# A new order of transposes and VectorE work in the first projection of a fused attention and MLP block, with its backward pass

## The chip, the cores and the metric

The kernel runs on one NeuronCore of a Trainium2 chip. The metric is device time in microseconds (us) of one launch. Engines are named as in the profile: PE is TensorE's matmul and PEld its weight load, DVE is VectorE, ACT is ScalarE, POOL is GpSimd, and SP is SyncE, which here only issues transfers (DMAs).

## The reference

The reference computes a transformer block's output and, from `grad_out`, its gradients (seven outputs in all, bfloat16):

```
h   = x + A(layernorm(x))                 # linear attention, 32 heads of 20
h2  = h + B(layernorm(h))                 # SwiGLU MLP
A:  q, k, v = split(x @ wqkv);  phi(t) = where(t > 0, t + 1, exp(t)) + 1e-6
    o = phi(q) (phi(k)^T v) / (phi(q) sum_s phi(k));  A = o @ wo
B:  (silu(x @ w1) * (x @ w3)) @ w2
```

x is 2048 x 640, wqkv 640 x 1920, wo 640 x 640, w1 and w3 640 x 1728, w2 1728 x 640.

## The kernel before

The 2048 rows are 16 tiles of 128 rows (128 partitions). The 640 columns are 5 blocks of 128 (`DT`), or two halves of 320 (`HD`), since a PSUM bank holds 512 float32. All instructions are written out by hand in each engine's order; an engine takes its own list in order and waits on semaphores. So the order in which lines are called is the order on each engine, and an instruction that waits holds up all that stands behind it on its engine. SP's transfers are also one list in order.

**Stage 1 (0 to 55 us)**, around which the change lies, goes over tiles t = 0 to 15:

- layer norm statistics on DVE (`Stats.part`: two BatchNorm statistics, L147, an aggregate, L150, an addition of epsilon, L153), then 1/sigma on POOL (L154);
- normalization in place: on DVE (L160), or for tiles 10, 12 and 14 on ACT (`norm_act`, L165), which needs a bias that POOL makes (L169, L170);
- the transposed rows `pqT`: for tiles 0 to 7 by five PE transposes into PSUM (L254) and an ACT copy (L256), for tiles 8 to 15 by a transposing DMA on SP (L247);
- the key product, 2 x 5 matmuls of 320 columns into a two-bank PSUM tile "big" (L260), of which there are two buffers;
- phi: Exp (L277) and Relu (L278) on ACT from PSUM, and two DVE operations (L281, L282), put off in the list `held` (the "rest").

Between the tiles stand four query products (`q_tile`, after the tiles in `QT`), four chunks of the MLP's backward product (`ghh_chunk`, 5 matmuls of 512 columns, L371, with an ACT copy, L391), and the accumulation of phi(k)^T x (`m_part`, L402). Before the first rows arrive, PE runs 44 matmuls on ones (L441). Loads are issued in the order of the lines 114, 187 to 193 and 429 to 435: x tiles 0 and 1, two weight blocks, x tiles 2, 3, 4 to 7, then `w2T`, `g2T`, `w2T`, x tiles 8 to 11, the query weights, x tiles 12 to 15. During the loop, stores of keys and normalized rows (`outs`) and MLP weights (`trickle`) go into SP's list too.

**Stage 2 (to about 88 us)** ends the sums, transposes the matrix M by DMA (L414), finishes queries and makes the combined matrix Wp. **Stage 3 (88 to 100 us)** computes the attention output of the tiles 0 to 3 (and 4) in halves: `f2_half(t, j)` is 5 matmuls (L586), for the second half one more with x (L584), an addition on DVE (L591) or a copy on ACT (L589), and the second layer norm's statistics; `f2_hn(t)` normalizes on DVE, `f2_ht(t)` transposes on PE (L677) and copies on ACT. Their order is the list in `run(...)`, lines 801 to 809. After that come the MLP, the backward pass and the weight gradients, up to 825 us, which the change leaves alone.

Of the kernel before, what the change touches and what calls it, by code (L numbers as in the profile page):

```python
# [9 lines left out]
P = 128  # L10
BF16 = mybir.dt.bfloat16
F32 = mybir.dt.float32
ALU = mybir.AluOpType
AF = mybir.ActivationFunctionType
# [4 lines left out]
S, D, H, F = 2048, 640, 32, 1728  # L19
DH = D // H  # L20
ST, DT = S // P, D // P
# [3 lines left out]
HD = D // 2  # L25
# [30 lines left out]
def kernel(  # L56
# [51 lines left out]
    cp = pool("cp")  # L108
# [4 lines left out]
    x_sb = x_ext[:, :, 0:D]  # L113
# [16 lines left out]
    class Stats:  # L130
# [25 lines left out]
        def center(self, out, src, t):  # L156
            V.tensor_scalar(out=out, in0=src, scalar1=self.mv[:, t, 0:1], scalar2=None, op0=ALU.subtract)
# [4 lines left out]

        def norm_act(self, out, src, t):

            A.activation(out=out, in_=src, func=AF.Identity, bias=self.nb[t][:, 1:2], scale=self.rs[:, t:t + 1])  # L165

        def bias(self, t):
            nb = self.nb[t] = cp.tile([P, 2], F32, name="nb", bufs=4)
            G.tensor_tensor(out=nb[:, 0:1], in0=self.mv[:, t, 0:1], in1=self.rs[:, t:t + 1], op=ALU.mult)  # L169
            G.tensor_tensor(out=nb[:, 1:2], in0=zero[:], in1=nb[:, 0:1], op=ALU.subtract)  # L170

    ln1, ln2 = Stats("ln1"), Stats("ln2")

# [7 lines left out]
    def load_wq(a, b):  # L181
        dma(out=wqkv[:, :, a * HD:b * HD], in_=wq_v[:, :, a * HD:b * HD])

    def load_x(a, b):
        dma(out=x_sb[:, a:b, :], in_=xS[:, a:b, :])

    load_x(1, 2)
    A.activation(sg[:], zero[:], AF.Exp)
    load_wq(2, 3)
    load_wq(3, 4)  # L190
    load_x(2, 3)
    load_x(3, 4)
    load_x(4, 8)

# [26 lines left out]
    def load_g2T(c):  # L221
        g2T[c] = U2.tile([P, DT, W], BF16, name="g2T", tag="g2T", bufs=2)
        dmaT(out=g2T[c][:], in_=goD[c * W:(c + 1) * W, :])

    def load_w13(c0, c1):
        def go1():
            dma(out=w1[:, c0:c1, 0:F], in_=rows(B_w1)[:, c0:c1, :])

        def go3():
            dma(out=w3[:, c0:c1, :], in_=rows(B_w3)[:, c0:c1, 0:F - FL])  # L230
        return [go1, go3]
# [3 lines left out]
    Z = cp.tile([P, DT], F32, name="Z")  # L235

    XT_DMA = 8
    WARM = 44

    def on_act(t):  # L240
        return t > XT_DMA and t % 2 == 0

    def p1_norm(t):
        xn = x_sb[:, t, :]
        (ln1.norm_act if on_act(t) else ln1.norm)(xn, xn, t)
        if t >= XT_DMA:
            dmaT(out=pqT[:, :, t * P:(t + 1) * P], in_=xn)  # L247

    def p1_tr(t, parts=((0, DT),)):
        xn = x_sb[:, t, :]  # L250
        for a, b in parts:
            tr = ps.tile([P, DT, P], BF16, name="tr", bufs=2)
            for c in range(a, b):
                T.transpose(tr[:, c, :], xn[:, c * P:(c + 1) * P], ident[:])  # L254

            A.copy(out=pqT[:, a:b, t * P:(t + 1) * P], in_=tr[:, a:b, :])  # L256

    def p1_half(acc, t, n0):
        for c in range(DT):
            T.matmul(acc, lhsT=pqT[:, c, t * P:(t + 1) * P], rhs=wqkv[:, c, n0:n0 + HD], start=(c == 0),  # L260
                     stop=(c == DT - 1))

    def p1_mm(t, n0):
        acc = ps.tile([P, 2, 512], F32, name="big", bufs=2)
        for j in range(2):
            p1_half(acc[:, j, 0:HD], t, n0 + j * HD)
        return acc

    def two(ap):
        return ap.rearrange("p (j n) -> p j n", j=2)  # L270

    held = []

    def phi(acc, dst, then=None):

        mq, rq = (p1.tile([P, D], BF16, name=n, bufs=b) for n, b in (("mq", 3), ("rq", 3)))
        A.activation(two(mq[:]), acc[:, :, 0:HD], AF.Exp)  # L277
        A.activation(two(rq[:]), acc[:, :, 0:HD], AF.Relu)  # L278

        def rest():  # L280
            V.tensor_scalar(out=mq[:], in0=mq[:], scalar1=1.0, scalar2=1e-6, op0=ALU.min, op1=ALU.add)  # L281
            V.tensor_tensor(out=dst, in0=mq[:], in1=rq[:], op=ALU.add)  # L282
            if then is not None:
                then()
        held.append(rest)

    def phi_rest(keep=0):
        while len(held) > keep:
            held.pop(0)()
# [13 lines left out]

    def q_tile(t):
        q_home(t)
        phi(p1_mm(t, 0), pqs[t])

    dz = {}

# [65 lines left out]
    def ghh_chunk(n, acc):  # L375

        c, fc = divmod(n, FT)
        if fc == FT - 1:
            gh, hw = ghh[n // 2], W // 2
            G.memset(gh[FL:, 1, :], 0.0)  # L380
            for d in range(DT):
                for h in range(2):
                    T.matmul(acc[h * FL:(h + 1) * FL, 0:hw], lhsT=w2T[:, d, fc * P:fc * P + FL],
                             rhs=g2T[c][:, d, h * hw:(h + 1) * hw], start=(d == 0), stop=(d == DT - 1))
            for h in range(2):
                A.copy(out=gh[:FL, 1, h * hw:(h + 1) * hw], in_=acc[h * FL:(h + 1) * FL, 0:hw])
            return
        mm5_to(acc, w2T, fc, g2T[c])
        if n % 2 == 0:
            ghh[n // 2] = pf.tile([P, 2, W], BF16, name="ghh", bufs=4)  # L390
        A.copy(out=ghh[n // 2][:, n % 2, :], in_=acc[:])  # L391
# [37 lines left out]
    def load_w2T(a, b):  # L429
        dmaT(out=w2T[:, :, a:b], in_=B_w2[a:b, :])  # L430

    zero_pads()
    load_w2T(0, 2 * P)
    load_g2T(0)
    load_w2T(2 * P, 4 * P)
    load_x(8, 12)
    load_wq(0, 2)
    load_x(12, ST)
    warm = ps.tile([P, 512], F32, name="warm", tag="tr", bufs=2)
    for _ in range(WARM):  # L440
        T.matmul(warm[:, 0:P], lhsT=ones[:], rhs=ones[:], start=True, stop=True, skip_group_check=True)  # L441
    ln1.run(x_sb, 0, 1)
    ln1.part(x_sb, 1, 0)
    for a, b in ((0, 2 * P), (2 * P, D)):
        ln1.norm(x_sb[:, 0, a:b], x_sb[:, 0, a:b], 0)
    p1_tr(0, ((0, 2), (2, DT)))
    for t in (1, 2):
        if t == 1:
            ln1.part(x_sb, t, 1)
            p1_norm(t)  # L450
            ln1.run(x_sb, t + 1, t + 2)
        else:
            ln1.part(x_sb, t + 1, 0)
            p1_norm(t)
    ln1.part(x_sb, 3, 1)
    w13 = [go for c0, c1 in ((0, 2), (2, 4), (4, 5)) for go in load_w13(c0, c1)]
    w13 += [lambda: dma(out=w1[:, :, F:FP], in_=rows(B_w3)[:, :, F - FL:F])]

    def load_wo():
        dma(out=wo[:], in_=A_wo.rearrange("(c p) n -> p c n", p=P))  # L460

    trickle = {3: w13[0], 4: w13[1], 11: lambda: load_wq(4, 6), 12: w13[2], 14: w13[3], 15: load_wo}

    stat_of = {t: (t + 4,) for t in range(7)}
    stat_of.update({7: (11, 12), 8: (13,), 9: (14,), 10: (15,)})
    norm_of = {t: (t + 3,) for t in range(8)}
    norm_of.update({8: (11, 12), 9: (13,), 10: (14,), 11: (15,)})

    def xn_out(g, q):
        sl = slice(g * TPC, (g + 1) * TPC)  # L470
# [3 lines left out]
        sl = slice(g * TPC, (g + 1) * TPC)  # L474
        dma(out=pk_v[:, sl, :], in_=pk_all[:, sl, :])

    outs = {6: ((group_out, 0),), 7: ((xn_out, 0, dma),), 10: ((group_out, 1), (xn_out, 1, dma)), 13: ((group_out, 2),)}

    QT = (5, 7, 9, 11)
    for t in range(ST):  # L480
        k = p1_mm(t, D)
        if t < 3:
            p1_tr(t + 1, ((0, 2), (2, DT)))
        for n in stat_of.get(t, ()):
            ln1.run(x_sb, n, n + 1)
            if on_act(n):
                ln1.bias(n)
        for n in norm_of.get(t, ()):
            if not on_act(n):
                p1_norm(n)  # L490
        phi_rest(t < 4)
        phi(k, pk_all[:, t, :])
        for n in norm_of.get(t, ()):
            if on_act(n):
                p1_norm(n)
        if t in QT:
            q_tile(QT.index(t))
        if 2 <= t < 6:
            ghh_chunk(t - 2, ps.tile([P, 2, 512], F32, name="gp", tag="big", bufs=2)[:, 0])
            p1_tr(t + 2)  # L500
        if t >= 3:
            m_part(0, [t - 3])
        if t >= 11:
            V.memset(bd[:, t - 11, :], 0.0)
            make_mask(t - 11)
        if t >= 9:
            m_part(1, [2 * (t - 9), 2 * (t - 9) + 1])
        for f, *n in outs.get(t, ()):
            f(*n)
        if t in trickle:  # L510
            trickle[t]()
# [285 lines left out]
    def kv3():  # L797
# [4 lines left out]
        (q_late, 12, lambda: (f2_wT(0), f2_wT(1))), (q_late, 13, lambda: (f2_wT(2), f2_wT(3))), (phi_rest,),  # L802
        (q_late, 14, lambda: f2_wT(4)), (load_x, 4, 8), (r_head, 5), (r_prod, 7), (r_store, 5, 6), (f2_m_out,),
        (f2_w_out,), (q_out, 8, 10), (q_out, 10, 14), (load_w2T, 8 * P, 10 * P), (mlp_ghh, 4), (q_late, 15),
        (sig_table,), (f2_half, 0, 0), (f2_half, 1, 0), (f2_half, 0, 1), (f2_half, 1, 1), (f2_hn, 0), (mlp_ghh, 5),
        (f2_half, 2, 0), (f2_hn, 1), (load_w2T, 10 * P, F), (f2_half, 2, 1), (f2_ht, 0), (f2_half, 3, 0), (f2_hn, 2),
        (f2_half, 3, 1), (f2_ht, 1), (mlp_ghh, 6), (f2_hn, 3), (f2_ht, 2), (r_red, 6), (r_inv, 6), (r_scale, 6), (r_T, 6),
        (f2_half, 4, 0), (f2_ht, 3), (mlp_ghh, 7), (f2_half, 4, 1), (r_red, 7), (r_inv, 7), (r_scale, 7), (r_T, 7),
        (r_store, 6, 8))
    p1.release()  # L810
# [623 lines left out]
```

## Time and profile before

| what | value |
|---|---|
| median of 5 runs | 826.6 us (826.46 to 827.25) |
| profiled execution, its own time | 826.57 us |
| its span (first to last instruction) | 824.8 us |
| PE busy | 817.1 us, 99% of the span |
| DVE, ACT, POOL busy | 453.7, 318.9, 134.1 us |
| PE busy in 0:5, 5:10, 10:15, 15:20 us | 3.88, 4.42, 3.70, 5.00 us |
| PE busy in 70:80, 80:90, 90:100 us | 9.77, 9.72, 9.19 us |
| granted PE clock | 0.999 of full speed |

The page's busy times are sums over one profiled execution. The windows give the busy time of each engine in a stretch, counted from the start of the span. A line of the timeline holds the start, the length, the engine, the line of the kernel, the operation, what it writes and reads, how often, and in brackets the idle time of the engine before it with what ended it. A "SPq" line is the issue of a transfer, not the transfer itself; the transfer view gives the time from issue to landing.

### The profile page before, as it was taken

The numbers are of one execution on the slowest core, as the hardware profiler recorded it, in microseconds if no ns is written. First come the engines' busy times: TensorE is split into PE (matmuls) and PEld (weight loads), VectorE is DVE, ScalarE is ACT, GpSimd is POOL, SyncE is SP. The second block draws the span as 40 slices with busy tenths as digits, with TensorE's granted clock in tenths as the row PEclk, the third lists the DMA queues.
The fourth block names the chain that finished last, engine by engine and source line by source line (L and its number), as shares of the span: only waits on it lengthen the run. The fifth ranks groups of instructions, "written<-read, shape, count | busy, mean of one in ns | idle before, by whom it ended". The sixth has DMA issues, their size and how long they took to land.

```text
span 824.8 us, 14217 instructions
## 1 busy us (share of the span) xinstructions
PE 817.1 (99%) x5551; PEld 523.0 (63%) x5551; DVE 453.7 (55%) x960; ACT 318.9 (39%) x609; POOL 134.1 (16%) x196
## 2 busy tenths in 40 slices
PE   8999999999999999999999999999999999999998
PEld 5677644555555555777777777777777777555554
DVE  7859897999898566300057777772681545200000
ACT  5855787655655666011121212222212334211111
POOL 2334343223323212100001111110220000000000
PEclk9999999999999999999999999999999999999999
DMA  9899999696484555999878889258995788985781
GB/s 265 206 319 210 247 243 283 201 237 170 123 223 128 151 190 167 214 248 265 222 166 182 193 214 200 59 111 178 247 235 93 164 189 176 217 201 132 162 173 38
DMA packets 318338, 157.58 MB, mean 191 GB/s; under 512 B 235456, under 2 KB 311456, under 8 KB 318272
## 3 DMA queue, kind: packets, MB, share of 16 engines
q1 hardware_dynamic: 286256, 120.65, 63.5%
q0 software_dynamic: 7376, 24.81, 8.9%
q10 hardware_dynamic: 24640, 11.23, 6.6%
q8 instruction: 43, 0.70, 0.4%
q14 instruction: 23, 0.19, 0.1%
HBM read 48.15 MB, written 51.46 MB: 121 GB/s over the span
## 4 chain that ended last, share of the span: by engine, by line
PE 94%; DMA 2%; DVE 1%; SPq 1%; ACT 1%; POOL 1%; issue 0%; DVEq 0%; ACTq 0%
PE mm L371 20%; PE job L1198 19%; PE ghn L1000 14%; PE gxn L1356 8%; PE o L766 7%; PE gw L955 7%; PE big L260 3%; PE gwo L1085 3%; PE gr L1057 3%; PE dkv L1302 3%; PE macc L402 2%; PE at L586 2%; DMA g2T<-in_grad_out_dram 1%; DMA mT<-mbs 1%; PE dkv L1230 1%; PE gp L371 1%
## 5 line engine op out<-in xcount | busy, mean ns | idle before, releaser
L1198 PE MATMUL job<-gb,hnN 128*128 128x432 bf16 (+2 forms) x656 | 117.0, 342 | 0.0
L1000 PEld LDWEIGHTS <-ggb 128*128 128x128 bf16 x864 | 84.5, 98 | 32.8
L1198 PEld LDWEIGHTS <-hnN 128*128 128x128 bf16 x656 | 63.6, 98 | 53.4
L371 PE MATMUL mm<-pqT,w 128*128 128x512 bf16 x405 | 93.6, 379 | 0.0
L371 PEld LDWEIGHTS <-w 128*128 128x128 bf16 x540 | 52.5, 98 | 62.9 <-issue 0.8
L1202 ACT CAST obs<-job 128x432 bf16<-128x432 f32 (+3 forms) x61 | 29.3, 480 | 123.1 <-PE job L1198 123.1
L766 PE MATMUL o<-w,hhT 128*128 128x320 bf16 x448 | 67.5, 299 | 0.0
L1000 PE MATMUL ghn<-w13a,ggb 128*128 128x320 bf16 x448 | 63.5, 299 | 0.0
L1000 PE MATMUL ghn<-w13b,ggb 128*128 128x320 bf16 x416 | 61.4, 299 | 0.0
L371 PE MATMUL mm<-g2T,w2T 128*128 128x512 bf16 x240 | 59.6, 379 | 0.0
L766 PEld LDWEIGHTS <-hhT 128*128 128x128 bf16 x448 | 43.8, 98 | 23.6
L955 PE MATMUL gw<-g,hb 128*128 128x320 bf16 x416 | 56.8, 299 | 0.0
L1065 POOL TENSOR_TENSOR sz<-Zb,g_h 128x640 f32<-128x640 bf16 x16 | 20.2, 1260 | 199.4 <-DVE g_h L1063 199.4
L955 PEld LDWEIGHTS <-hb 128*128 128x128 bf16 x416 | 40.6, 98 | 16.0 <-issue 0.3
L1356 PE MATMUL gxn<-wqT,gT 128*128 128x320 bf16 x320 | 48.7, 299 | 0.0
L391 ACT CAST ghh<-mm 128x512 bf16<-128x512 f32 x48 | 28.2, 588 | 46.9 <-PE mm L371 41.4
L705 ACT ACTIVATE sig<-mm 128x512 bf16<-128x512 f32 x56 | 33.5, 599 | 27.3 <-PE mm L371 23.9
L1012 ACT ACTIVATE gs<-ghn 128x640 bf16<-128x640 f32 x16 | 11.2, 703 | 79.1 <-PE ghn L1000 79.1
L371 PEld LDWEIGHTS <-w2T 128*128 128x128 bf16 x260 | 25.3, 98 | 24.6 <-issue 1.4
L260 PE MATMUL big<-wqkv,pqT 128*128 128x320 bf16 x260 | 39.5, 299 | 0.9 <-ACT pqT L256 0.6
L260 PEld LDWEIGHTS <-pqT 128*128 128x128 bf16 x320 | 30.4, 98 | 14.1 <-ACT pqT L256 2.1
L1356 PEld LDWEIGHTS <-gT 128*128 128x128 bf16 x320 | 31.3, 98 | 12.2
(201 smaller groups left out, 1283.0 us busy)
## 6 DMA issues: line engine op xcount, KB each, us to landing
hh_d<-hhT SPq DMA_DIRECT2D x24, 256.0 KB, 2.6
gg_d<-gate POOLq DMA_DIRECT2D x24, 256.0 KB, 4.0
gg_d<-ghh POOLq DMA_DIRECT2D x24, 256.0 KB, 3.4
ggb<-gg_d SPq DMA_DIRECT2D x6, 896.0 KB, 5.5
ggb<-gg_d SPq DMA_DIRECT2D x6, 832.0 KB, 7.0
x_sb<-in_A_x_dram SPq DMA_DIRECT2D x7, 640.0 KB, 6.1
out_dram<-obs ACTq DMA_DIRECT2D x39, 108.0 KB, 3.2
ggb<-gg_d SPq DMA_DIRECT2D x2, 1728.0 KB, 13.2
```

The source lines that it names most:

```text
L260: T.matmul(acc, lhsT=pqT[:, c, t * P:(t + 1) * P], rhs=wqkv[:, c, n0:n0 + HD], start=(c == 0), stop=(c == DT - 1))
L371: T.matmul(acc[:], lhsT=w[:, c, fc * P:(fc + 1) * P], rhs=rhs[:, c, :], start=(c == 0), stop=(c == DT - 1))
L391: A.copy(out=ghh[n // 2][:, n % 2, :], in_=acc[:])
L705: A.activation(sig[:, i, :], gp[:], AF.Sigmoid)
L766: T.matmul(o2["ps"][:, 0:HD], lhsT=hhT[c][:, fc, i * P:(i + 1) * P], rhs=w2[:, fc, j * HD:(j + 1) * HD], start=(fc == 0), stop=(fc == FT - 1))
L955: T.matmul(acc[:, j, 0:HD], lhsT=hb[b][:, t, i * P:(i + 1) * P], rhs=g2[:, t, j * HD:(j + 1) * HD], start=(t == 0), stop=(t == ST - 1))
L1000: T.matmul(acc[:, j, 0:HD], lhsT=ggb[t // 2][:, k, lo:lo + P], rhs=rhs[:, j * HD:(j + 1) * HD], start=(k == 0), stop=(k == NG - 1))
L1057: T.matmul(gr[t][:, j, 0:HD], lhsT=ghT[t][:, c, :], rhs=wT2[:, c, j * HD:(j + 1) * HD], start=(c == 0), stop=(c == DT - 1))
L1085: T.matmul(acc[m][:, j, 0:n], lhsT=r_sb[:, t, m * P:(m + 1) * P], rhs=g_hx[:, t, j * HD:j * HD + n], start=(t == 0), stop=(t == ST - 1))
L1198: T.matmul(acc[:, 0:n], lhsT=lhs[:, t, m * P:(m + 1) * P], rhs=rhs(t), start=(t == 0), stop=(t == ST - 1))
L1202: A.copy(out=ob, in_=acc[:, 0:n])
L1356: T.matmul(acc[:, j, 0:HD], lhsT=g, rhs=wqT[:, k, j * HD:(j + 1) * HD], start=(k == 0), stop=(k == 14))
```

## The change

It does the following, in the order of the program:

1. x tile 2 is loaded before the second weight block, x tiles 8 to 11 before the second part of `w2T`.
2. 34 instead of 44 matmuls on ones at the start, and 8 more between the transposes and the product of tile 0.
3. Tile 0 is only centered at first (`RAW = 1`), 256 columns on DVE and 384 on ACT; its 1/sigma is applied as the scale of Exp and Relu, and to the rows themselves later (`("C", 0)` at step 3).
4. The transposes of tile t + 1 stand between the two halves of the key product of tile t, and are copied in one piece.
5. DVE's work in the loop follows a written list `v_steps`: S is statistics, N a normalization (A one on ACT), R the oldest put-off rest of phi, C the scaling of tile 0.
6. The chunks of the MLP's backward product move from the steps 2 to 5 to the steps 3 to 6, and into the PSUM banks of tag "m"; `m_part(0, ...)` starts at step 7 with tiles 0 to 2.
7. The second stores of keys and of rows go out at step 12 instead of 10, behind the last transposing DMAs; the first MLP weights one step later; the first query product at step 6.
8. The bias for normalization on ACT is one POOL instruction instead of two.
9. In stage 3, the first halves of the tiles 0 to 2 come first, and all halves of the tiles 0 to 3 before the first transposes.

```diff
-            G.tensor_tensor(out=nb[:, 0:1], in0=self.mv[:, t, 0:1], in1=self.rs[:, t:t + 1], op=ALU.mult)
-            G.tensor_tensor(out=nb[:, 1:2], in0=zero[:], in1=nb[:, 0:1], op=ALU.subtract)
+            G.tensor_scalar(out=nb[:], in0=self.mv[:, t, 0:1], scalar1=self.rs[:, t:t + 1], scalar2=-1.0, op0=ALU.mult,
+                            op1=ALU.mult)
...
+    load_x(2, 3)
     load_wq(3, 4)
-    load_x(2, 3)
...
-    WARM = 44
+    WARM = 34
+    RAW = 1
...
+    def p1_scale(t):
+        xn = x_sb[:, t, :]
+        V.tensor_scalar(out=xn, in0=xn, scalar1=ln1.rs[:, t:t + 1], scalar2=None, op0=ALU.mult)
...
+    def p1_mm(t, n0, between=None):
+        acc = p1_acc()
         for j in range(2):
             p1_half(acc[:, j, 0:HD], t, n0 + j * HD)
+            if j == 0 and between is not None:
+                between()
...
+        kw = dict(scale=ln1.rs[:, t:t + 1]) if t < RAW else {}
+        A.activation(two(mq[:]), acc[:, :, 0:HD], AF.Exp, **kw)
+        A.activation(two(rq[:]), acc[:, :, 0:HD], AF.Relu, **kw)
...
+    load_x(8, 12)
     load_w2T(2 * P, 4 * P)
-    load_x(8, 12)
...
+    def center_first():
+        V.tensor_scalar(out=nmean[:], in0=ln1.mv[:, 0, 0:1], scalar1=-1.0, scalar2=None, op0=ALU.mult)
+        center(0, 0, 2 * P)
+        A.activation(out=x_sb[:, 0, 2 * P:], in_=x_sb[:, 0, 2 * P:], func=AF.Identity, bias=nmean[:, 0:1])
...
+    ln1.part(x_sb, 0, 0)
+    ln1.part(x_sb, 0, 1, center_first)
     p1_tr(0, ((0, 2), (2, DT)))
+    warm_up(8, p1_acc()[:, 0])
+    stat(1)
+    ln1.part(x_sb, 2, 0)
+    p1_norm(1)
+    ln1.part(x_sb, 2, 1)
+    ln1.part(x_sb, 3, 0)
+    p1_norm(2)
+    ln1.part(x_sb, 3, 1)
+    ln1.part(x_sb, 4, 0)
+    p1_norm(3)
+    ln1.part(x_sb, 4, 1)
...
-    trickle = {3: w13[0], 4: w13[1], 11: lambda: load_wq(4, 6), 12: w13[2], 14: w13[3], 15: load_wo}
+    trickle = {4: w13[0], 5: w13[1], 11: lambda: load_wq(4, 6), 12: w13[2], 14: w13[3], 15: load_wo}
+    R = None
+    v_steps = {1: (R, ("N", 4)), 2: (("S", 5), R, ("N", 5)), 3: (("S", 6), R, ("N", 6), ("C", 0)),
+               4: (("S", 7), R, ("N", 7), ("S", 8)), 5: (R, ("N", 8), ("S", 9)), 6: (R, ("N", 9), ("S", 10)),
+               7: (("S", 11), R, R, ("A", 10), ("N", 11)), 8: (("S", 12), R, R, ("S", 13), ("A", 12)),
+               9: (("N", 13), R, ("S", 14)), 10: (R, R, ("S", 15), ("A", 14)), 11: (("N", 15), R)}
...
-    outs = {6: ((group_out, 0),), 7: ((xn_out, 0, dma),), 10: ((group_out, 1), (xn_out, 1, dma)), 13: ((group_out, 2),)}
-    QT = (5, 7, 9, 11)
+    outs = {6: ((group_out, 0),), 7: ((xn_out, 0, dma),), 12: ((group_out, 1), (xn_out, 1, dma)), 13: ((group_out, 2),)}
+    QT = (6, 7, 9, 11)
+    M0 = {7: (0, 1, 2), 8: (3, 4, 5)}
+    M0.update({t: (t - 3,) for t in range(9, ST)})
     for t in range(ST):
-        k = p1_mm(t, D)
-        if t < 3:
-            p1_tr(t + 1, ((0, 2), (2, DT)))
+        k = p1_mm(t, D, (lambda: p1_tr(t + 1)) if t + 1 < XT_DMA else None)
...
-        if 2 <= t < 6:
-            ghh_chunk(t - 2, ps.tile([P, 2, 512], F32, name="gp", tag="big", bufs=2)[:, 0])
-            p1_tr(t + 2)
-        if t >= 3:
-            m_part(0, [t - 3])
+        if 3 <= t < 7:
+            ghh_chunk(t - 3, ps.tile([P, 512], F32, name="gp", tag="m", bufs=2))
+        m_part(0, M0.get(t, ()))
...
-        (sig_table,), (f2_half, 0, 0), (f2_half, 1, 0), (f2_half, 0, 1), (f2_half, 1, 1), (f2_hn, 0), (mlp_ghh, 5),
-        (f2_half, 2, 0), (f2_hn, 1), (load_w2T, 10 * P, F), (f2_half, 2, 1), (f2_ht, 0), (f2_half, 3, 0), (f2_hn, 2),
-        (f2_half, 3, 1), (f2_ht, 1), (mlp_ghh, 6), (f2_hn, 3), (f2_ht, 2), (r_red, 6), (r_inv, 6), (r_scale, 6), (r_T, 6),
+        (sig_table,), (f2_half, 0, 0), (f2_half, 1, 0), (f2_half, 2, 0), (f2_half, 0, 1), (f2_half, 1, 1), (f2_hn, 0),
+        (f2_half, 2, 1), (f2_half, 3, 0), (f2_half, 3, 1), (f2_ht, 0), (f2_hn, 1), (mlp_ghh, 5), (load_w2T, 10 * P, F),
+        (f2_hn, 2), (f2_ht, 1), (mlp_ghh, 6), (f2_hn, 3), (f2_ht, 2), (r_red, 6), (r_inv, 6), (r_scale, 6), (r_T, 6),
```

## The prediction

> **What bounds the kernel now.** I read the page's busy times first, then TensorE's waits over the whole run, then the windows in which the change acts.
>
> ```profile
> PE 817.1 (99%) x5551; PEld 523.0 (63%) x5551; DVE 453.7 (55%) x960; ACT 318.9 (39%) x609; POOL 134.1 (16%) x196
> ...
> PE   8999999999999999999999999999999999999998
> ```
>
> TensorE (PE) is busy 817.1 of 824.8 us. So only its 7.7 us of idle time, and work taken from it, can be won. About 1.1 us lie before its first matmul and 3.3 us behind its last, and the change touches neither. The rest, about 3.3 us, lies in two places, which the windows show (the column behind the length is PE's busy time):
>
> ```profile
> 5.00:10.00 5.00, 4.42 (x37) 2.47 (x35) 3.70 (x12) 2.42 (x6) 1.21 (x3) 1.00 1.15 310
> 10.00:15.00 5.00, 3.70 (x28) 1.89 (x27) 4.79 (x16) 4.28 (x9) 1.91 (x3) 1.00 1.13 237
> 15.00:20.00 5.00, 5.00 (x40) 3.40 (x39) 4.61 (x16) 3.55 (x6) 1.36 (x2) 1.00 0.99 344
> ...
> 90.00:100.00 10.00, 9.19 (x72) 5.87 (x72) 8.22 (x25) 5.55 (x12) 4.78 (x8) 1.00 0.98 294
> ```
>
> From 100 to 800 us PE has no idle at all: what is won before 100 us reaches the end. The timeline of PE names the stalls:
>
> ```profile
> 6.30 1.96 PE L260 MATMUL big<-wqkv,pqT 128*128 128x320 bf16 x10
> 8.09 0.44 PE L254 MATMUL tr<-ident,x_sb 128*128 128x128 bf16 x5
> 8.83 1.64 PE L260 MATMUL big<-wqkv,pqT 128*128 128x320 bf16 x10 [0.30 <-ACT pqT L256]
> 10.31 0.45 PE L254 MATMUL tr<-ident,x_sb 128*128 128x128 bf16 x5
> 11.05 1.64 PE L260 MATMUL big<-wqkv,pqT 128*128 128x320 bf16 x10 [0.30 <-ACT pqT L256]
> ...
> 14.15 1.24 PE L371 MATMUL gp<-g2T,w2T 128*128 128x512 bf16 x5 [0.98 <-DMA g2T<-in_grad_out_dram]
> ```
>
> The reader sees a key product (10 matmuls) start every 2.22 us, because each waits for ScalarE (ACT) to copy its transposed rows, and then a wait for g2T. A matmul's modelled record outlives its issue, so I count by starts: 0.136 us a 320-column matmul, 0.056 a transpose, 0.215 a 512-column one, which are the steps between starts here.
>
> **Part 1: the first tile.** Before, VectorE (DVE) waits for GpSimd's 1/sigma (0.57 us) and normalizes at 5.14. Now it only subtracts the mean, at about 4.4 behind the aggregate (4.06 + 0.21), 0.31 us for 256 columns as in L160's half: 4.7. The 34 remaining warm-ups end at 1.12 + 34 x 0.107 = 4.75. The other 384 columns go to ACT, an operation without a row: between 0.42 (128x320 cast) and 0.92 us (L165, 128x640); I take 0.64. Copies of the transposes end near 6.1 (6.4 at the upper end). Nothing is won: the first weights were issued at 1.73 and land 4.5 us later, at 6.24, and the product began at 6.30 for that reason. It begins at 6.30 again; the 8 new fillers lie in that wait, cost 0.
>
> The spacing of the 44 warm-ups in the trace is 0.107 us for 34 steps and 0.056 after 4.8 us. The Trainium skill, "TensorE: Matmul & The Clock Gate", Part 1, says that the gate opens after about 3.4 us of activity in a free-running window, give or take 0.5 us, and not after a count; that speaks against a fixed 34. By it, a gate open 0.5 us late would slow two transposes and the fillers, all still before 6.30: the sum stays.
>
> **Part 2: tiles 1 to 3.** The load of x tile 2 moves ahead of the second weight block. It landed at 7.80 (issue 2.76 + 5.0); the step from a tile's landing to the next is 0.44, so I put it at 6.24 + 0.43 = 6.67 and the weights at 7.80 (before 7.38). This matters, since in DVE's order half of tile 2's statistics now stand ahead of tile 1's normalization: statistics 6.73, norm 7.13 to 7.57, transposes of tile 1 at 7.62 (inside product 0), second half 7.90 to 8.58, ACT's 640-column copy (0.70) to 8.82, product 1 at 8.88 (before 8.83). From there a tile costs one loop: half a product 0.68, transposes 0.28, their drain 0.17, copy 0.70, two handovers of 0.05: 1.93 against 2.22. Products 2 and 3 start at 10.82 and 12.76; product 3 with its transposes ends at 14.40. The chunk that waited for g2T (it lands at 14.02) is now behind product 3 and waits no more: it ends at 15.48. Before, the same work (products 0 to 3, transposes 1 to 4, one chunk) was issued by 15.51 + 1.36 = 16.87. **Won: 1.39 us.**
>
> **Part 3: tiles 4 to 15.** PE's work is the same, only ordered anew. Two waits of before, 0.23 at 24.4 and 0.32 at 32.56 us (weight loads held by the PSUM buffer that ACT still read), lie in this stretch. New is this: ACT's normalization of tiles 10, 12 and 14 stands right behind the Exp and Relu of keys 7, 8 and 10, and its statistics come only one step earlier in DVE's list. For tile 12: its statistics started at 29.57 and now stand behind two more finishing pairs (0.32 + 0.49 each) and norm 11 (0.36), all 1.39 earlier: 30.2. They take 1.3 with the epsilon, 1/sigma 0.55 to 32.1, bias 0.40 to 32.5, then 0.92 on ACT; Exp and Relu of key 9 (0.60 apart, 0.70 each) end at 34.72. They are queued behind it, and product 10 needs their PSUM buffer: it starts at 34.76, where PE is ready at 34.35. Tile 14 does the same to product 12: 0.27. With 0.08 at query 0, new waits are 0.76 against 0.55. Product 12 starts at about 40.75 against 41.82: **1.07 won so far.**
>
> The bias is now one GpSimd tensor-scalar, which no row shows: 0.19 and 0.40 are the rows of a 128x1 tensor-tensor there, 1.26 that of 128x640. I take 0.40, the nearest under load. At 0.19 all these waits shrink by about 0.2 in sum; at 1.26 they cost some 1.0 more.
>
> The transfers of tiles 8 and 9: before, w1 lands at 14.66 + 11.9 = 26.6 and w3 at 15.88 + 12.8 = 28.7; a transposed row transfer takes about 0.6 behind them. Tile 8's now stands ahead of w3: 27.2 against product 8 at 28.6. Tile 9's stands behind it: 29.9 against 30.8. Both covered, the second by 0.9. The second stores of keys and rows leave the queue at step 10 and come after the four last transposes: nobody reads them before 100 us; but the weights behind them (w1, w3, wo) then start with as much ahead of them as before. The scaling of row tile 0 (0.44 on DVE at step 3) lies under the chunk.
>
> **Part 4: 50 to 88 us** is unchanged work, one stretch of it waiting on a transfer:
>
> ```profile
> 61.37 2.07 SPq L414 DMA_TRANSPOSE mT<-mbs  x1
> 63.55 2.60 SPq L361 DMA_TRANSPOSE pqT<-pq  x1
> 66.20 3.06 SPq L430 DMA_TRANSPOSE w2T<-in_B_w_dram  x1
> 69.36 2.85 SPq L361 DMA_TRANSPOSE pqT<-pq  x2
> 72.31 2.06 SPq L414 DMA_TRANSPOSE mT<-mbs  x1
> ```
>
> SP issues these back to back up to the mT transfer that PE waits for at 78.16 (0.23 us). The first started on data (ACT's copy ended at 61.34), and SP was free at 60.75: it can come 0.62 earlier, not 1.07. So between 0 and 0.45 is given back; I take 0.2.
>
> **Part 5: attention halves.** The order becomes 0a 1a 2a 0b 1b 2b 3a 3b, then the transposes. Third a-half (0.68) covers the wait for Wp (0.28 at 89.89). Worked on the old clock: halves from 87.96, four of 0.68 and four of 0.816: 93.94; transposes of row 0 and a chunk to 95.30. DVE is the slow side: adds at 88.84, 89.77, 90.70 (0.93 each with its statistics), then statistics of 0 and 1, norm 0 at 93.29, statistics of 2, add of 3 at 94.46, statistics to 96.28, and only then norm 1 (0.43), which stood at 94.51 before: 96.63. PE waits 1.38 there, and is at row 3's transposes at 99.00. Before:
>
> ```profile
> 99.05 0.45 PE L677 MATMUL trh<-ident,hn 128*128 128x128 bf16 x5 [0.81 <-DVE hn L160]
> ```
>
> Won: 0.05. The stalls move, their sum hardly changes.
>
> **Sum.** 1.07 - 0.2 + 0.05 = 0.9, taken from the profiled execution's own 826.57 us (span 824.8 and 1.8 around it; the median of the five runs is 826.6, so the two agree): 825.6 us.
>
> **Rivals.** *More is won* (824.6): GpSimd is faster in the waits of part 3 (0.55 and 0.19 us, rows that stand where DVE is not in its fast copies), which removes most of 0.76, and mT moves with PE. *Nothing* (825.6 + 1.1 = 826.7): x tile 2 lands as late as before, 7.80. Then product 1 starts at 10.0, 1.1 later, as DVE's order puts tile 1 behind it. For it: wide weight rows share all DMA engines; against: loads landed in issue order. A bias of 1.26 gives the same (826.6). *Slower* (827.4): the clock. PE is idle 0.3, 0.5 and 0.6 us between 4.75 and 7.62, and the fast warm-ups of before are gone; if the clock fell to half for one stretch as long as the first, 3.6 us, it would lose 1.8. It decides when matmuls between 6.3 and 10 us start 0.27 apart instead of 0.136. Against: before, the clock stayed up through 1.2 us without a matmul start (12.95 to 14.15). *The change does not do what it says*: if tile 1's transposes wait past the second half, the loop stays at 2.22, 0.9 is lost: counted under nothing.
>
> **Chances.** Forecast (825.0 to 826.0) 0.40; more (825.0 and below) 0.36; nothing (826.0 to 827.0) 0.15; slower (827.0 and up) 0.09. The range 824.0 to 827.2 takes in the bounds of the bias, of mT and of the late tile. The line at 0.2% (1.65 us, about what a measurement of this kernel can tell from no change) lies at 824.95 and 828.25: faster is the "more" case, 0.36; slower is most of the last, 0.07; within, 0.57.
>
> **What would show it.** Product 1 near 8.9 and then starts 1.9 apart; no wait for g2T; ACT idle about 1 us ahead of the norms of 12 and 14, and a wait of 0.4 and 0.3 at products 10 and 12; PE's largest wait at the second attention transposes, 1.4. Wrong if product 1 starts after 9.5, if the matmuls before 10 us are half as fast, or if PE waits for pqT transfers or over 0.7 for mT.

## The result, and the profile after

The changed kernel is slower: 827.03 us (median of 44 runs, 825.37 to 838.0) against 826.86 (79 runs, 826.0 to 835.0). The ratio of the mean times, without the slowest run, is 1.0030, 95% interval 1.0017 to 1.0042; the 0.2% that the forecast called measurable lies inside that interval. The median hides the shape: 27 runs lie at 825.4 to 827.9 us with a median of 826.3, 0.6 us under the kernel before, and 17 lie at 831.7 to 838.0, around 834.7. Before, one of the 79 runs was over 830.

The profiled run is one of the lower group: 825.76 us, span 824.0. Its busy time, and the windows that were shown of before (the column behind the length is PE's busy time):

```profile
PE 816.4 (99%) x5549; PEld 523.2 (63%) x5549; DVE 453.5 (55%) x961; ACT 320.6 (39%) x607; POOL 133.5 (16%) x193
```

```profile
5.00:10.00 5.00, 4.05 (x39) 2.83 (x38) 3.89 (x13) 2.55 (x6) 1.54 (x3) 1.00 1.17 299
10.00:15.00 5.00, 4.32 (x37) 2.84 (x35) 4.45 (x16) 4.97 (x8) 1.37 (x3) 1.00 1.06 239
15.00:20.00 5.00, 5.00 (x39) 3.20 (x37) 4.76 (x15) 4.48 (x9) 0.99 (x3) 1.00 1.09 305
...
90.00:100.00 10.00, 8.75 (x68) 5.55 (x67) 9.40 (x28) 5.61 (x11) 4.12 (x7) 1.00 1.02 315
```

From 5 to 20 us PE is busy 0.25 us longer than before, from 90 to 100 us 0.44 shorter. PE's timeline shows the places:

```profile
6.06 0.84 PE L265 MATMUL big<-wqkv,pqT 128*128 128x320 bf16 x5
7.34 0.45 PE L255 MATMUL tr<-ident,x_sb 128*128 128x128 bf16 x5 [0.44 <-DVE x_sb L160]
8.24 1.52 PE L265 MATMUL big<-wqkv,pqT 128*128 128x320 bf16 x10 [0.44 <-DMA wqkv<-in_A_wqkv_dram]
...
11.29 0.85 PE L265 MATMUL big<-wqkv,pqT 128*128 128x320 bf16 x5 [0.58 <-ACT pqT L257]
...
14.86 1.24 PE L380 MATMUL gp<-g2T,w2T 128*128 128x512 bf16 x5
```

```profile
95.95 0.45 PE L701 MATMUL trh<-ident,hn 128*128 128x128 bf16 x5 [1.25 <-DVE hn L160]
...
98.28 0.44 PE L701 MATMUL trh<-ident,hn 128*128 128x128 bf16 x5
```

The chunk of g2T waits no more. In the attention one wait of 1.25 us at the second row's transposes stands in place of the two of before, and the fourth row's transposes start at 98.28 instead of 99.05. So this run shows what was forecast (825.6). Part of that is luck: it is the third fastest of the 44, and its group's median lies 0.6 us under the kernel before, not the 0.9 of the forecast. The result is decided by something that it does not show: the upper group.

### The profile page after: what moved, and what is told of

Same layout as the page of the kernel before. It is cut to its first block, busy times and chain, and to the rows that moved or that the text cites. A ratio compares the mean times of both kernels' runs of the same rounds, so it can differ in the third digit from the quotient of the medians.

```text
span 824.0 us, 14214 instructions
## 1 busy us (share of the span) xinstructions
PE 816.4 (99%) x5549; PEld 523.2 (63%) x5549; DVE 453.5 (55%) x961; ACT 320.6 (39%) x607; POOL 133.5 (16%) x193
## 4 chain that ended last, share of the span: by engine, by line
PE 96%; DVE 2%; ACT 1%; DMA 1%; issue 0%; SPq 0%; POOL 0%; DVEq 0%; ACTq 0%
PE mm L380 20%; PE job L1222 19%; PE ghn L1024 14%; PE gxn L1380 8%; PE o L790 7%; PE gw L979 7%; PE big L265 3%; PE gwo L1109 3%; PE gr L1081 3%; PE dkv L1326 3%; PE macc L411 2%; PE at L610 2%; PE mm L265 1%; DMA wqkv<-in_A_wqkv_dram 1%; DVE st L147 1%; PE dkv L1254 1%
```

## The experiments

Kernels were run beside the kernel before, which stayed at 826.0 to 829.4 in 129 of its 134 runs there; the other five took 830.4 to 836.0, so it knows long runs too, but rarely. Sixteen runs in three theories follow.

**First theory: the clock at the start.** The upper group's mean granted clock is 0.993 to 0.998. PE is idle in places between 4.75 and 8.2 us, so full speed might be granted late. Four runs tell this from the two rivals (the new 1.25 us wait, the order of the loads).

```diff
-    WARM = 34
+    WARM = 44
```

> The changed kernel with 44 instead of 34 matmuls on ones. Of the 44 runs of the changed kernel 27 took 825.4 to 827.9 us and 17 took 831.7 to 838.0 with a mean granted clock of 0.993 to 0.998. Theory (start clock): full speed is granted only after a stretch of dense PE work, and with 34 matmuls on ones the idle places from 4.75 to 8.2 us fall into that stretch in part of the runs. Then ten more fill it to about 5.8 us and no run takes over 830; median 826.3, within 0.4 us of the changed kernel's undisturbed runs, since the first 1.0 us of them lies in the wait for tile 1's rows. Rival A (the new 1.25 us wait of PE at 96 us lets the clock fall): 4 of 10 runs stay at 834 to 835. Rival B (loads in another order, the idle places at 7 and 8 us alone): also 4 of 10 stay.

Measured: 830.64 us (828.2 to 832.8, 9 runs), ratio 1.0043 (1.0029 to 1.0057). The opposite: no run under 828.

```diff
-    WARM = 34
+    WARM = 24
```

> The changed kernel with 24 instead of 34 matmuls on ones. Theory (start clock): PE has idle time from 3.7 us on, so nearly all runs (over 7 in 10) take 832 or more, and the trace shows PE at half speed behind 5 us for a long stretch, some 8 us lost in all. Rival A (wait at 96 us) and rival B (idle places at 7 and 8 us): 4 in 10 as in the changed kernel, median near 826.5 or 834 by luck; by A the half-speed stretch stands behind 95 us, by B between 8 and 20 us.

Measured: 826.8 to 835.2, 7 of 12 over 830. In the profiled run (828.5 us, not one of the seven) full speed begins at 4.3 us and stays.

Old order of the halves, the list of `run(...)` as before:

```diff
-        (sig_table,), (f2_half, 0, 0), (f2_half, 1, 0), (f2_half, 2, 0), (f2_half, 0, 1), (f2_half, 1, 1), (f2_hn, 0),
+        (sig_table,), (f2_half, 0, 0), (f2_half, 1, 0), (f2_half, 0, 1), (f2_half, 1, 1), (f2_hn, 0), (mlp_ghh, 5),
...
```

> The changed kernel with the order of the attention halves of before. Theory (start clock): still about 4 in 10 runs at 832 or more; the others at 826.2 to 826.4, 0.1 us either way of the changed kernel, since the waits there only moved (forecast 0.05 us for the order; the trace shows 1.25 us at row 1 against 0.28 and 0.81 before). Rival A (the new 1.25 us wait at 96 us drops the clock): no run over 830.

Measured: 8 of 12 over 830. The order of the halves is not the cause. The profiled run, 832.6 us, fell into the upper group and ended the theory: full speed from 4.2 us, then a wait of 5.11 us for the normalization of row tile 3 (DVE, L160) at 98 us, and behind it one stretch of half speed, from 103.15 us, 3.41 long.

And the kernel before with fewer matmuls on ones:

```diff
-    WARM = 44
+    WARM = 34
```

> The kernel before with 34 instead of 44 matmuls on ones, nothing else changed. Theory (start clock): its PE is then idle from 4.77 to 5.5 us, so runs at 832 or more appear here too, fewer than in the changed kernel since its first product starts at 6.3 and runs through to 8.1: 1 to 4 in 10; the others at 826.8. Rivals A and B: none, all 826.0 to 828.0 but for 2 in 79.

Measured: 827.2 us, 1 of 12 over 830: as before, within what can be told (ratio 1.0004, 0.9981 to 1.0027).

**Second theory: a late transfer.** `f2_hn(3)` writes its rows into a buffer of tag "pql", the one that query tile 5 (`pql`) left. Its transposing transfer to `pqT` (issued on SP, L370) must have read it first. In the trace of before it landed at 97.48 us and the normalization started at 98.54, so nothing waited. In the run with the old order of the halves it landed at 102.42. The changed kernel again, as it is:

> The changed kernel once more on the chip of the other runs, to see both of its groups beside them: about 6 in 10 runs at 825.4 to 827.9 and 4 in 10 at 832 to 838. If the profiled run falls into the upper group, late transfer theory: tile 3's normalization on VectorE stands still for over 3 us up to a landing of the query transfer behind 100 us, and the half-clock window follows it; start clock theory (already doubtful): half speed before 20 us.

Measured: 8 of 12 over 830 (833.5 us). The profiled run is of the upper group, 835.49 us. Its VectorE and PE timelines, and the tile view of pqT from 86 to 106 us (who waited for it, and the time from issue to landing):

```profile
94.77 0.80 DVE L160 TENSOR_SCALAR hn<-x_sb,ln_mv,ln_rs 128x640 bf16<-128x640 bf16 x2
105.00 0.45 DVE L160 TENSOR_SCALAR hn<-x_sb,ln_mv,ln_rs 128x640 bf16<-128x640 bf16 x1 [9.43 <-DMA pqT<-pql]
```

```profile
96.92 0.84 PE L610 MATMUL at<-Wp,pqT 128*128 128x320 bf16 x5
105.51 0.72 PE L701 MATMUL trh<-ident,hn 128*128 128x128 bf16 x5 [7.75 <-DVE hn L160]
106.02 2.34 PE L380 MATMUL mm<-g2T,w2T 128*128 128x512 bf16 x5
```

```profile
  DVE hn L160: 9.4, 1
...
DMA to landing us min/median/max: 16.7/16.7/16.7
```

The transfer takes 16.7 us instead of 7.2 (lower group) and 8.1 (before). The windows of PE behind it (busy, then granted clock, DMA share, GB/s):

```profile
100.00:103.00 3.00, 0.00 (x0) 0.99 1.16 226
103.00:106.00 3.00, 0.49 (x5) 0.50 1.30 106
106.00:109.00 3.00, 3.00 (x12) 0.50 1.05 127
109.00:112.00 3.00, 3.00 (x14) 0.87 1.20 304
```

The clock is at half from 102.96 to 109.79 us; a chunk takes 2.34 us instead of 1.24. PE works in it from 105.51 on, so it loses half of 4.28 us: 2.1. Row 3's transposes start 7.2 us later than in the lower group's profiled run (105.51 against 98.28), and with the 2.1 that is 9.4 of the 9.7 us by which this run is longer. The clock falls 5 us after PE has begun to wait: it is a consequence, not the cause.

If so, an early transfer removes the upper group, and a late one makes it the rule:

```diff
-        (q_late, 14, lambda: f2_wT(4)), (load_x, 4, 8), (r_head, 5), (r_prod, 7), (r_store, 5, 6), (f2_m_out,),
+        (q_late, 14, lambda: f2_wT(4)), (r_head, 5), (load_x, 4, 8), (r_prod, 7), (r_store, 5, 6), (f2_m_out,),
```

> The changed kernel with the transposing transfer of query tile 5 (pqT from pql) issued on SP ahead of the load of x tiles 4 to 7 instead of behind it. The start clock theory fell with the runs before. New theory (late transfer): the second normalization's output of tile 3 takes the buffer that this transfer reads; where the transfer lands late, at 102.4 or 102.5 instead of 95.7 to 97.5 us, VectorE's normalization and PE behind it stand still for 3.4 to 5.2 us, and the clock then falls for a 3.4 us window (1.7 us more). Issued some 0.7 us earlier and ahead of 640 KB, it lands by 93: no run over 829, median 826.0 to 826.4. Rival (the stall has another cause, and the late transfer is beside it): 4 in 10 runs stay at 832 to 836.

Measured: 827.17 us, 825.78 to 828.07 in 11 runs, none above; the transfer landed at 93.34. The group is gone, but the median is 0.8 us over the expected range. The profiled run took 827.76 us and has a stretch of half clock at 7.4 us, shown further below.

```diff
-        (load_x, 4, 8), (r_head, 5), ... (load_w2T, 8 * P, 10 * P),
+        (load_x, 4, 8), (r_red, 5), (r_inv, 5), (r_scale, 5), ... (load_w2T, 8 * P, 10 * P),
+        (lambda s=pqs[5]: dmaT(out=pqT[:, :, 5 * P:6 * P], in_=s),),
```

> The changed kernel with the same transfer issued behind the transposing load of w2T, so late on purpose: SP is free there at 96.6 us, so it lands at 101 to 103 in every run. Late transfer theory: normalization 3 starts at about 102.5 instead of 96.3 and the third attention transposes on PE at 103 instead of 98.3, 4.7 us, plus 1.7 for one window at half clock: all runs at 831 to 835, none under 830. Rival (another cause): two groups as in the changed kernel, at 826 and at 834.

Measured: 833.8 us, all 6 runs at 831.6 to 841.0; it landed at 102.20 and the normalization followed:

```profile
102.33 0.45 DVE L160 TENSOR_SCALAR hn<-x_sb,ln_mv,ln_rs 128x640 bf16<-128x640 bf16 x1 [5.88 <-DMA pqT<-pql]
```

**Why late, and why only now?** First, whether the new order of the halves (part 9 of the change, alone, in the kernel before) does it:

```diff
-        (sig_table,), (f2_half, 0, 0), (f2_half, 1, 0), (f2_half, 0, 1), (f2_half, 1, 1), (f2_hn, 0), (mlp_ghh, 5),
+        (sig_table,), (f2_half, 0, 0), (f2_half, 1, 0), (f2_half, 2, 0), (f2_half, 0, 1), (f2_half, 1, 1), (f2_hn, 0),
...
```

> The kernel before with the new order of the attention halves alone. With the run that had the old order in the changed kernel this makes a square of four. Theory (cover): the new order asks for normalization 3 some 2 us earlier (96.3 instead of 98.5), so the transfer has less cover; a landing at 97.5 as in the trace of before costs up to 1 us in part of the runs; late landings (over 830 us) in 1 to 3 of 10 runs at most, since the stage before is the old one. Otherwise 826.6 to 827.0. Rival (the new first stage alone makes the transfer late): as before, no run over 830.

Measured: 826.94 us, 826.2 to 827.5 in 11 runs, ratio 0.9998 (0.9990 to 1.0007). It does not: the upper group comes with the new first stage (the run with the old order of the halves), though that ends 30 us earlier.

What differs at 88 us is the distance between two queues: the list of stores on GpSimd starts 0.94 us earlier than before, the transfer on SP 0.82. The first big store (`m_d`) was issued 0.22 to 0.42 us behind the transfer in the three profiled runs with the old first stage and the old order on GpSimd, and none was late. In the eight with the new first stage, this order on GpSimd and SP's order unchanged, it was issued between 0.51 us ahead of the transfer and 0.17 behind. Four of these landed late, at 102.4 to 104.9 us (0.02 ahead; 0.08, 0.09 and 0.15 behind), and four in time, at 95.7 to 96.8 (0.51, 0.17 and 0.16 ahead; 0.17 behind). So the distance is smaller in all eight, but it does not tell the late ones from the others.

The trace's packet records show what a late one looks like. In the lower group's profiled run the transfer's 640 packets of 256 bytes all moved between 92 and 94 us. In the upper group's, 355 packets of that size moved in these two microseconds. Eight packets of the stores, begun from 92.6 us on, stood still until 95.1 to 97.3, four of 256 bytes on SP's queue with them from 93.5 to 95.2, and then that queue went on at 38 to 81 such packets per us up to 100 us (the next transposing load has packets of the same size, so not all need be the transfer's). The last column of the windows (GB/s over all queues) tells the same, first of the lower group's profiled run, then of the upper's:

```profile
94.00:96.00 2.00, 0.75 (x5) 0.15 (x3) 1.90 (x7) 0.99 (x2) 0.80 (x2) 1.00 0.97 373
```

```profile
94.00:96.00 2.00, 0.88 (x9) 0.50 (x9) 1.50 (x6) 0.82 (x2) 0.68 (x1) 1.00 0.52 63
```

The third theory was the **lead**: the transfer is late when the big stores (1.9 MB) are ahead of it. The three runs in time with the store ahead speak against it in this form. It was tried first in the kernel before:

```diff
-        ... (r_prod, 7), (r_store, 5, 6), (f2_m_out,),
-        (f2_w_out,), (q_out, 8, 10), (q_out, 10, 14), (load_w2T, 8 * P, 10 * P), ...
+        ... (r_prod, 7), (f2_m_out,),
+        (f2_w_out,), (q_out, 8, 10), (q_out, 10, 14), (r_store, 5, 6), (load_w2T, 8 * P, 10 * P), ...
```

> The kernel before with the store of query tile 5 behind the four other stores of that place on GpSimd, so that these, 1.8 MB, start about 1 us earlier. The lead of the first store over the transposing transfer was 0.17 to 0.36 us in the three traces with the old first stage (none late), and 0.41 to 0.74 in five traces with the new one (three late). Theory (lead): with a lead of about 1.2 us the transfer falls behind the stores on the DMA engines here too: 3 to 9 of 10 runs at 830 to 836, normalization 3 behind 100 us. Rival (something else of the new first stage makes it late): 826.0 to 828.4 as before, or a few tenths more, as normalization 3 has cover up to 98.5 us.

Measured: 831.5 us, 828.5 to 835.0, 4 of 6 over 830, and the same picture with the old first stage:

```profile
102.22 0.45 DVE L160 TENSOR_SCALAR hn<-x_sb,ln_mv,ln_rs 128x640 bf16<-128x640 bf16 x1 [3.57 <-DMA pqT<-pql]
```

(The small store of tile 5 moved too and reads the same buffer; it landed at 102.02, the transfer at 102.09. Both were late, and this run can't part them. PE also waited 1.6 us for Wp in it, instead of 0.3.) Then the big stores were put off in the changed kernel, by one GpSimd instruction in front of them:

```diff
-        ... (r_store, 5, 6), (f2_m_out,),
+        ... (r_store, 5, 6), (lambda: G.memset(p1.tile([P, D], BF16, name="rq", bufs=3)[:], 0.0),), (f2_m_out,),
```

> The changed kernel with one more GpSimd instruction (a memset of 128x640, at most 1.3 us by the 64x640 one's 0.63) ahead of the four big stores, so that these start about 1 us later and the transposing transfer of query tile 5 has the lead. It costs up to 0.7 us, as 1/sigma of tile 0 comes later. Theory (lead of the stores): at most 1 of 10 runs over 830, the rest at 826.3 to 828.0. Rival (the lead is not what makes it late): 4 of 10 or more over 830, as in the changed kernel.

Measured: 826.48 us, 825.2 to 827.4, none of 12 over 830. The memset took 0.65 us, less than expected and enough: the first big store was issued 1.16 us behind the small one instead of 0.58, and 0.25 us behind the transfer, as in the kernel before. So a later start of the big stores takes the upper group away. That it does so by the order of issue is not shown: with the same memset, in the version with the better order below, the store came 0.02 us behind the transfer, and this landed at 96.19.

**Is the buffer the only way to PE?** Two runs gave row tile 3 another buffer. First in a query tile's space:

```diff
+        own = [p1.tile([P, D], BF16, name="hn", tag="mq", bufs=3) for _ in range(3)] if t == 3 else None
-        hn[t] = (pf.tile([P, D], BF16, name="hn", tag="pql", bufs=4) if 2 <= t < TPC else
+        hn[t] = own[2] if own else pf.tile([P, D], BF16, name="hn", **(dict(tag="pql", bufs=4) if t == 2 else dict(bufs=2)))
```

> The changed kernel with a buffer of its own for the second normalization's output of tile 3, in space that a query tile has left; no transfer is moved. Late transfer theory: the transposing transfer of query tile 5 lands late in part of the runs as before, but nobody waits for it: VectorE starts the normalization at 96.3 us in every run, PE's only wait there is the 1.25 us at the second transposes, no run is over 829, median 826.0 to 827.2. Rival (stores and loads in that stretch hold up PE or VectorE in another way too): part of the runs still over 830, with another wait on PE behind 98 us.

Measured: 832.1 us, 7 of 10 over 830. This proves nothing about the theory, since the edit made a wait of its own: ScalarE's second sigmoid result of the MLP takes that space and now waits for the store of those very rows (the profiled run, of 827.86 us, has 1.5 us of waits behind ScalarE). Then in a free part of the query buffer:

```diff
-        hn[t] = (pf.tile([P, D], BF16, name="hn", tag="pql", bufs=4) if 2 <= t < TPC else
+        hn[t] = (pkx[0][:, DT + 6, :] if t == 3 else
...
-    pkx.append(p1.tile([P, DT + 6, D], BF16, name="pkx", tag="pk"))
+    pkx.append(p1.tile([P, DT + 7, D], BF16, name="pkx", tag="pk"))
```

> The changed kernel with the second normalization's output of tile 3 in a part of the query buffer that nobody uses any more. The run before put it into a query tile's space, which ScalarE's second sigmoid result of the MLP takes at about 102 us: so that wrote a new wait, for the store of the normalized rows (it landed at 104.7 in the profiled run, PE waited 1.5 us behind ScalarE), and its upper group proves nothing. Here the next user of the space comes behind 107 us. Late transfer theory: normalization 3 starts at 96.3 us in every run, no run over 829.5, median 826.0 to 827.2. Rival (late loads and stores of that stretch hold PE up through others too): 3 or more of 10 runs over 830, with another wait on PE.

Measured: 826.9 us; 9 of 12 at 826.0 to 827.3, 3 at 830.0 to 831.5. The profiled run is one of the three. Its transfer landed at 104.50, and row tile 3's transposes (now out of `pkx`) did not wait, but something later did:

```profile
98.48 0.44 PE L701 MATMUL trh<-ident,pkx 128*128 128x128 bf16 x5
...
117.47 2.29 PE L380 MATMUL mm<-g2T,w2T 128*128 128x512 bf16 x5 [2.21 <-ACT gate L731]
```

ScalarE waits there for VectorE and for a store of `gate`: the backlog reaches PE by another way, for 2.2 us, and again a 3.4 us stretch at half clock follows. So the buffer is not the only way: without it the three upper runs still cost 3 to 5 us instead of 8. (One run of the table below with this buffer took 835.4 us; it was not traced.)

**A better version.** The 1.25 us wait comes from `(f2_hn, 1)` standing behind both halves of row tile 3 on DVE:

```diff
-        (f2_half, 2, 1), (f2_half, 3, 0), (f2_half, 3, 1), (f2_ht, 0), (f2_hn, 1), (mlp_ghh, 5), (load_w2T, 10 * P, F),
+        (f2_half, 2, 1), (f2_hn, 1), (f2_half, 3, 0), (f2_half, 3, 1), (f2_ht, 0), (mlp_ghh, 5), (load_w2T, 10 * P, F),
```

With the early transfer, with the free buffer, with the memset, and with the last two:

> The changed kernel with two edits: the transposing transfer of query tile 5 ahead of the x load, which took away the upper group, and the second normalization of tile 1 on VectorE ahead of the first half of tile 3 instead of behind both its halves. Theory: its 1.25 us wait on PE at the second transposes goes, up to 0.45 us comes back at the third, so 0.8 to 1.0 us less than the 825.8 to 828.1 (median 827.2) with the first edit alone: median 826.2, no run over 829, and 0.1% below the kernel before. Rival (the waits only move, as the change of the order did): median 827.0 to 827.2, with a wait of about 1 us at the third or fourth transposes.

> The same with the normalization of tile 1 on VectorE ahead of both halves of tile 3, as a candidate to beat both kernels. If the upper group is gone and the 1.25 us wait at the second transposes too: median 825.0 to 826.2, 0.1 to 0.2% under the kernel before, no run over 829. If only the order helps: two groups, the lower at 824.5 to 826, the upper at 832 to 836.

> The changed kernel with the memset ahead of the four big stores (0.65 us, 12 of 12 runs at 825.2 to 827.4) and with the normalization of tile 1 ahead of both halves of tile 3. Theory (lead): the transfer keeps its lead, no run over 829; the 1.25 us wait at the second transposes goes and 0.2 to 0.4 comes back at the third: median 825.4 to 825.8, 0.15% or more under the kernel before. Rival (the run with the memset was a lucky dozen): 3 or more of 10 runs over 830, as normalization 3 has no more cover than in the changed kernel.

> The same with the second normalization's output of tile 3 in the free part of the query buffer as well, so that no buffer waits for the transfer. If the lead decides that it is late, the free buffer adds nothing: median and spread as in the run beside it, 825.4 to 825.8, none over 829. If late transfers still come, they cost less here (up to 4 us) than there (8 us).

| run | median (range), runs | over 829.5 us | ratio to before |
|---|---|---|---|
| early transfer | 826.8 (824.5 to 832.1), 12 | 3 | 1.0008 (0.9991 to 1.0025) |
| free buffer | 826.6 (825.0 to 835.4), 12 | 3 | 1.0002 (0.9976 to 1.0029) |
| memset | 825.55 (824.7 to 826.2), 12 | 0 | 0.9973 (0.9955 to 0.9990) |
| memset, free buffer | 825.5 (824.6 to 829.5), 12 | 0 | 0.9977 (0.9957 to 0.9998) |

The order pays about 0.9 us in all (825.55 against 826.48 with the memset alone), and 36 of 36 runs with the memset stay under 829.5, against 31 of 56 of the changed kernel. The free buffer adds nothing to the memset, and one run with both took 829.46, where none over 829 was expected. The third version beats both kernels: its slowest run, 826.2 us, lies under the median of the kernel before, 827.2 beside it, and under that of the changed kernel's lower group. PE's two waits there:

```profile
94.93 0.44 PE L701 MATMUL trh<-ident,hn 128*128 128x128 bf16 x5
...
96.75 0.45 PE L701 MATMUL trh<-ident,hn 128*128 128x128 bf16 x5 [0.29 <-DVE hn L160]
```

The early transfer with the same order missed: 3 of 12 went over 830. Its trace is of an undisturbed run. In the trace with the early transfer alone, the load of x, now behind, took 11.6 us instead of 4.9, but PE did not wait for it; what made the three runs slow was not shown.

## Why the prediction was wrong, point by point

| step | forecast | lower group's profile |
|---|---|---|
| Part 1, first key product | 6.30 us | 6.06; its second half waits 0.44 for weights |
| Part 2, products 1, 2, 3 | 8.88, 10.82, 12.76 | 8.91, 11.29, 13.21 |
| Part 2, chunk ends | 15.48 | 15.94: won 0.93, not 1.39 |
| Part 3, bias on GpSimd | 0.40 us | 0.26 to 0.46 |
| Part 3, ACT idle ahead of norms 12, 14 | about 1 us | 0.89 and 1.05 |
| Part 3, waits at products 10 and 12 | 0.41 and 0.27 us | 0.18 and 0.35, counted by starts |
| Part 3, product 12 | 40.75 (won 1.07) | 40.96 (won 0.86) |
| Part 4, given back to 88 us | 0.2 | 0.11 (halves at 87.21, before 87.96) |
| Part 5, second transposes wait | 1.38 | 1.25 |
| Part 5, won by the order | 0.05 | 0.02 |
| time | 825.6 | 825.76 |

- **Parts 1 to 3** were right in mechanism. Part 2 was 0.46 us too good: the loop of 1.93 us held from product 2 to 3 (1.92), but product 2 came 2.38 behind product 1, as it waited 0.58 for ACT's copy. The term that was off is the landing of the second weight block, put at 7.80 us: it came at about 8.2 (2.77 + 5.4), so the second half of product 0 began at 8.24 instead of 7.90. Its Exp and Relu, which stand ahead of tile 2's copy on ACT and have no term in the loop, kept ACT until 10.54, half a microsecond after the transposes of tile 2 had ended (9.59 + 0.44):

```profile
9.18 0.80 ACT L288 ACTIVATE mq<-big,ln_rs 128x640 bf16<-128x640 f32 x1 [0.65 <-PE big L265]
9.87 0.79 ACT L289 ACTIVATE rq<-big,ln_rs 128x640 bf16<-128x640 f32 x1
10.54 0.69 ACT L257 COPY pqT<-tr 128x640 bf16<-128x640 bf16 x1
```

  In Part 3 the sum has a slip: 1.39 less new waits of 0.76 against 0.55 is 1.18, not 1.07. It does not change the picture.
- **The step that failed** is in Part 5: "and is at row 3's transposes at 99.00". It dated the normalizations by VectorE's own work and 1/sigma, and never asked what their buffers wait for. Row tile 3's waits for the query transfer, which landed at 97.48 in the very trace that the forecast used, 1.06 us before it was needed (in the lower group's profile of the change 0.65: 95.69 against 96.34); a later landing was thus put at nothing, without a reason. In 25 of 56 runs the kernel now takes 5 us or more above the lower group's median. In the profiled one of them the transfer landed at 104.88 us, and PE, after a wait of 7.75 us, is at row 3's transposes at 105.51. The overall median, 827.03, does lie in the range of 824.0 to 827.2, but only because it falls at the edge between two groups: that is luck.
- **Behind it, Part 4**: "50 to 88 us is unchanged work". PE's was. But the forecast moved all behind it by one number, and SP's transfer and GpSimd's stores moved by 0.82 and 0.94. The runs show that the new first stage brings the late landings and that the start of the stores matters; that these 0.12 us are the link is not shown.
- **The rivals.** "Slower: the clock" named the right side, the wrong trigger and place. Its price was right per stretch: one run (827.76 us, of the early transfer) had it where the rival put it, at 7.4 to 10.8 us, behind a 1.37 us wait for weights, and a key product took 2.31 us instead of 1.52:

```profile
4.00:7.40 3.40, 1.64 (x23) 1.00 1.07 337
7.40:10.80 3.40, 3.40 (x16) 0.50 1.22 197
```

  But in the upper group it comes behind the wait at 97 us, and adds 2.1 to a stall of 7.75. No rival named a late transfer. The closing line has a sign, "if PE waits for pqT transfers", but the only such transfers that the prediction weighs are those of the tiles 8 and 9. So "slower" (827.0 and up) had 0.09; the median lies just in it, and 17 of 44 runs lie 4.7 us or more above its bound.
- **The weighing of the first tile's clock** held in the sum: "all still before 6.30" is true of the lower group's profile, in which the clock was at full speed from 5.69 us (before: 4.79). It is not true of every run: in two traces of later versions full speed began at 6.59 and 6.95 us.

What stays open: why packets of the stores stand still for up to 4 us, and what decides in a single run whether the transfer is caught by it. The memset and the new first stage change how often it is, and the order in which store and transfer are issued does not tell the runs apart.

## What to carry to other kernels

Date every buffer that a moved instruction writes, not only its inputs: list the transfers that still read it, with their landing in the trace, and distrust a small one: here a cover of 1 us over an 8 us transfer was none. When work is moved earlier, shift each queue by its own releaser and ask which transfers now start side by side. A single profile shows one draw: look at the spread of the runs before trusting a median, and test a suspected transfer by forcing it early and late.

## What the hardware showed that was not expected

- **Half-clock stretches come in one size.** They lasted 3.41 us in four profiled runs (old order of the halves, early transfer, stores first, free buffer) and 6.83 in two (late transfer, changed kernel again). The Trainium skill, "TensorE: Matmul & The Clock Gate", Part 1, gives a free-running window of 3,413 ns, after an idle one of which the clock falls to half; the traces agree with the length. They do not agree with "idle": in the window ahead of the fall at 7.4 us PE was busy 1.64 of 3.40 us, and with the free buffer 1.35 of the 3.41 us ahead of the fall at 117.32. The same section calls the ramp under 1% of a kernel's span; here one such stretch in which PE works costs 1.7 us, 0.2% of the span and almost twice what the change was to win.
- **Two queues stand still together.** Store packets of 5,120 bytes took up to 4.2 us each and packets of 256 bytes on SP's queue up to 1.7 in the same stretch; undisturbed, the first take about 0.2. The Trainium skill, "DMA: Bandwidth & Descriptors", Back-pressure in remote DMA, says that stalled writes stall the source engine's other queues too; the trace looks alike, though these are plain stores to DRAM and not remote ones, and which write stalled first is not shown.
- **Ten more matmuls on ones made it worse**: product 0 at 6.96 instead of 6.06 us, and at 828.2 or more in all 9 runs. In its one trace the same transfer landed at 102.53 us; where the other runs wait was not shown.
